# w_out in seven pairs by Strassen's products, its first fetches ahead of x's, block sums shared with GpSimd

## The chip, the cores and the metric

One core of one Trainium2 chip. The metric is the device time in microseconds of the program's one launch; lower is better. Engines are named as in the profile: PE (TensorE, matmuls), PEld (its weight loads), DVE (VectorE), ACT (ScalarE), POOL (GpSimd), SP (SyncE, which issues most DMAs).

## The reference

Talking-heads attention, and behind it a layer that normalizes `x @ w_in` and multiplies by `w_out`. The second half is what the change is about:

```
# q, k, v: 4 x 12 heads x 448 x 64; w_pre, w_post: 12 x 12
attn_out = attention(q, k, v, w_pre, w_post)
x = attn_out.transpose(0, 2, 1, 3).reshape(1792, 768)
h = x @ w_in                      # w_in: 768 x 1024
e = exp(h - max(h)); sm = e / sum(e)
solu = h * sm
ln = (solu - mean) / sqrt(var + 1e-6) * g_ln
out = ln @ w_out                  # w_out: 1024 x 768
```

All is float32 outside. Inside, a float32 matrix is the sum of two float16 ones, a high and a low half, and a product is three float16 matmuls (high x high, high x low, low x high).

## The kernel before, in words

The attention ends at about 430 us; its instructions stand in an order written by hand and are the same before and after the change. Behind it the program has 14 tiles of 128 tokens (`NT`), in the order of `TURNS` (11, 12, 13, 0 to 10), and seven pairs of tiles (`NPP`).

**Hidden product.** `hidden` (L1088) makes a tile's `x @ w_in` in 36 matmuls 128x512 into one of three PSUM banks `ps_h0` to `ps_h2`, tile t into bank t modulo 3. So tile 13 needs the bank of tile 10. VectorE takes a tile's maximum (L1711), ScalarE the exponent (L1722), VectorE the sum's reciprocal (L1733, L1736) and the product h x sm, `u` (L1739), which is the bank's last reader.

**Normalization.** ScalarE and small VectorE operations make the mean and the variance (L1751 to L1789), GpSimd a power (L1772). `ln_apply` (L1799, GpSimd) scales `u`, `ln_hi` (L1807, ScalarE) and `ln_lo` (L1811, GpSimd) split it into `lh` and `ll`, which go to DRAM (L1814) and come back transposed, `lt` (`turn`, L1826).

**w_out.** Eight fetches of 128 rows (`fetch_w_out`, DMA at L987) bring w_out as 64-bit words, issued by SP, between x's fetches `xf` (L974, L976). `convert_steps` turns each into float32: L1002, L1008, L1013, L1018 on VectorE, one step on ScalarE, the last, a product (L1021), on GpSimd. Then come maxima, one scale for all (`max_w_out`, `scale_w_out`), and the halves `wo_h` (ScalarE) and `wo_l` (VectorE, L377).

**Output product.** Of seven pairs, the first `NPL` = 2 are plain: four products of 24 matmuls 128x384 into banks `y`. The other five go by Strassen's algorithm: with both operands cut into 2 x 2 blocks, seven products of 12 matmuls replace eight blocks' worth, 84 in place of 96 a pair. For it VectorE adds the two halves of `lt` (`pair_whole`, L1841, `xs`), makes four block sums (`pair_sum`, L1854), and low halves (`part_lo`, L1663, `sz`); ScalarE makes the high halves. w_out's own block sums are `w_out_sum` (`tt`, `wo`) and their halves `tz`, also through the helper `minus` at L1663. `project` (L1903) issues the matmuls, into the `ps_h` banks for Strassen's products, and `emit` takes a product out of PSUM, scaled and added to what it belongs to (L1916 for the plain ones, L1935 for the others): nine VectorE operations and one on ScalarE a pair.

**What sets the order.** All of this is entered as tasks with engines, costs, due times and buffers (rings) into a planner, `moe`. `moe.order()` works greedily through them and its list is issued in that order, each engine's instructions in the order of the list. An instruction waits on its engine until what it reads is there.

Of the kernel before, what the change touches and what calls it, by code (L numbers as in the profile page):

```python
# [18 lines left out]
class Plan:  # L19
# [131 lines left out]
    def order(self):  # L151
# [94 lines left out]
def kernel(  # L246
# [748 lines left out]
    def convert_steps(dst, name):  # L995
# [24 lines left out]
        def product():  # L1020
            nc.gpsimd.tensor_tensor(out=dst, in0=z, in1=ex.bitcast(F32), op=ALU.mult)  # L1021
# [527 lines left out]
    with tc.manual_schedule():  # L1549
# [23 lines left out]
        wt_p = ctx.enter_context(tc.tile_pool(name="wt", bufs=1))  # L1573
        h_p = ctx.enter_context(tc.tile_pool(name="hp", bufs=2))
        cv_p = ctx.enter_context(tc.tile_pool(name="cv", bufs=2))
        lt_p = ctx.enter_context(tc.tile_pool(name="lt", bufs=2))
        sz_p = ctx.enter_context(tc.tile_pool(name="sz", bufs=2))
        ms_p = ctx.enter_context(tc.tile_pool(name="ms", bufs=3))
        ps_h = ctx.enter_context(tc.tile_pool(name="ps_h", bufs=1, space=PSUM))
        h_banks += [ps_h.tile([128, NF, 512], F32, name=f"ps_h{i}") for i in range(2)]  # L1580
        ps_y = ctx.enter_context(tc.tile_pool(name="ps_y", bufs=1, space=PSUM))
        ln_dr = [dram.tile([NT, 128, DFF], F16, name=f"ln_{z}") for z in "hl"]
# [10 lines left out]
        wo_h = wt_p.tile([128, KFF, DM], F16, name="wo_h")  # L1593
        wo_l = wt_p.tile([128, KFF, DM], F16, name="wo_l")
# [53 lines left out]
        NPP, NPL = NT // 2, 2  # L1648
        STEPS = [(i, j) for i in range(NPP) for j in range(4 if i < NPL else 7)]
# [575 lines left out]
```

## Time and profile before

| what | us |
|---|---|
| time, median of three runs | 636.11 |
| lowest and highest run | 635.67, 640.92 |
| the profiled execution's own time | 639.07 |
| its span on the core | 637.4 |

The profiled execution lies 2.96 us above the median; 1.67 us of it lie outside the span. Rows of the profile give a group's busy time, the mean duration of one instruction, and the idle time of its engine before it with the engine that ended it. In a row of the chain or of a timeline the first number is the start, the second the duration.

### The profile page before, as it was taken

The numbers are of one execution on the slowest core, as the hardware profiler recorded it, in microseconds if no ns is written. First come the engines' busy times: TensorE is split into PE (matmuls) and PEld (weight loads), VectorE is DVE, ScalarE is ACT, GpSimd is POOL, SyncE is SP. The second block draws the span as 40 slices with busy tenths as digits, with TensorE's granted clock in tenths as the row PEclk, the third lists the DMA queues.
The fourth block names the chain that finished last, engine by engine and source line by source line (L and its number), as shares of the span: only waits on it lengthen the run. The fifth ranks groups of instructions, "written<-read, shape, count | busy, mean of one in ns | idle before, by whom it ended". The sixth has DMA issues, their size and how long they took to land.

```text
span 637.4 us, 19852 instructions
## 1 busy us (share of the span) xinstructions
PE 607.9 (95%) x7674; PEld 409.0 (64%) x7674; DVE 542.8 (85%) x1293; ACT 453.1 (71%) x1022; POOL 289.8 (45%) x463
## 2 busy tenths in 40 slices
PE   7999989999899999999899998999999999999997
PEld 5757767777666776777577676764444445666664
DVE  4879988789797788997899898738999799999983
ACT  3879879998878888988799797625676688642110
POOL 2363584354673353862335426512678747510000
PEclk9999999999999999999899899999999999999999
DMA  8397288478877469889569762109994505571522
GB/s 195 117 203 222 97 179 228 158 197 202 236 176 185 167 187 186 252 194 230 181 189 197 235 215 90 37 4 347 273 249 112 148 35 132 157 176 50 115 79 72
DMA packets 135527, 106.81 MB, mean 168 GB/s; under 512 B 89508, under 2 KB 123400, under 8 KB 135432
## 3 DMA queue, kind: packets, MB, share of 16 engines
q1 hardware_dynamic: 129000, 91.36, 53.7%
q0 software_dynamic: 3712, 9.75, 6.3%
q10 hardware_dynamic: 2720, 4.42, 2.4%
q8 instruction: 61, 1.00, 0.7%
q14 instruction: 34, 0.28, 0.1%
HBM read 34.03 MB, written 16.97 MB: 80 GB/s over the span
## 4 chain that ended last, share of the span: by engine, by line
PE 63%; DVE 14%; DMA 7%; issue 5%; ACT 5%; POOL 4%; SPq 1%; POOLq 0%; DVEq 0%; ACTq 0%
PE ps_h L1088 13%; PE o L858 13%; PE ps_h L1903 11%; PE px L919 8%; PE ps L712 6%; PE pm L799 5%; PE y L1903 5%; DVE pm L811 4%; DVE s L735 3%; DMA sr<-s 2%; ACT e L827 2%; POOL wr L848 1%; DMA raw_v<-in_v_dram 1%; ACT s L730 1%; ACT p_t L381 1%
## 5 line engine op out<-in xcount | busy, mean ns | idle before, releaser
L858 PE MATMUL o<-wr,e 128*64 128x120 f32 x2520 | 161.3, 273 | 10.2 <-POOL wr L848 7.2
L858 PEld LDWEIGHTS o<-wr,e 128*64 128x64 f32 x2520 | 136.5, 138 | 44.3 <-POOL wr L848 23.5
L827 ACT ACTIVATE e<-pm,nb 128x448 f32<-128x448 f32 x180 | 114.6, 639 | 20.5 <-DVE pm L811 11.3
L811 DVE TENSOR_SCALAR_CACHE_REDUCE pm<-pm,c_nexp 128x448 f32<-128x448 f32 x171 | 113.5, 684 | 17.5 <-PE pm L799 15.3
L848 POOL TENSOR_SCALAR wr<-wq,sm 128x120 f32<-128x120 f32 x180 | 72.6, 411 | 105.3 <-DVE sm L842 66.7
L735 DVE SCALAR_TENSOR_TENSOR s<-ps,s 120x448 f16<-120x448 f32 (+1 forms) x180 | 105.7, 616 | 14.0 <-ACT s L730 11.5
L381 ACT COPY p_t<-o 128x480 f32<-128x480 f32 x180 | 107.8, 621 | 9.3 <-PE o L858 8.8
L730 ACT ACTIVATE s<-ps 120x448 f16<-120x448 f32 (+1 forms) x180 | 91.4, 551 | 21.0 <-PE ps L712 16.4
L919 PE MATMUL px<-p_t,raw_v 128*64 128x120 f32 (+3 forms) x1632 | 96.2, 259 | 0.3
L919 PEld LDWEIGHTS px<-p_t,raw_v 128*64 128x64 f32 x1632 | 83.6, 138 | 6.9 <-issue 6.0
L1088 PE MATMUL ps_h<-wi,xf 128*128 128x512 f16 x396 | 86.0, 379 | 0.8 <-DVE u L1739 0.8
L712 PE MATMUL ps<-k,q 64*64 64x448 f16 (+2 forms) x972 | 77.4, 355 | 6.1 <-DVE s L735 5.1
L1088 PEld LDWEIGHTS <-xf 128*128 128x128 f16 x396 | 38.8, 98 | 47.5 <-issue 1.1
L799 PE MATMUL pm<-sr,wp_hi 64*64 64x448 f16 (+1 forms) x684 | 56.5, 358 | 2.1 <-DMA sr<-s 1.6
L712 PEld LDWEIGHTS <-q 64*64 64x64 f16 (+2 forms) x972 | 33.4, 105 | 31.5 <-issue 21.1
L1903 PEld LDWEIGHTS <-lt 128*128 128x128 f16 x372 | 36.4, 98 | 24.2
L838 POOL TENSOR_SCALAR sm<-sm 128x2 f32<-128x2 f32 (+1 forms) x48 | 13.2, 276 | 69.4 <-ACT e L827 66.8
L827 ACT ACTIVATION_READ_ACCUMULATOR e<-pm,nb 128x1 f32 x180 | 37.3, 207 | 0.0
L1811 POOL TENSOR_TENSOR ll<-u,lh 128x1024 f16<-128x1024 f32 x14 | 32.0, 2284 | 11.4 <-ACT lh L1807 11.2
L377 DVE SCALAR_TENSOR_TENSOR xsl<-px,x_sc,xsh 128x120 f16<-128x120 f32 (+1 forms) x96 | 26.0, 326 | 12.4 <-ACT xsh L372 12.3
L799 PE MATMUL pm<-sr,wp_lo 64*64 64x448 f16 (+1 forms) x342 | 36.2, 349 | 0.0
L1903 PEld LDWEIGHTS <-sz 128*128 128x128 f16 x240 | 23.5, 98 | 15.5
(241 smaller groups left out, 1040.2 us busy)
## 6 DMA issues: line engine op xcount, KB each, us to landing
sr<-s SPq DMA_DIRECT2D x176, 210.0 KB
cv_wi<-in_moe_w_in_dram SPq DMA_DIRECT2D x24, 256.0 KB
cv_wo<-in_moe_w_out_dram SPq DMA_DIRECT2D x8, 768.0 KB
raw_k<-in_k_dram POOLq DMA_DIRECT2D x18, 224.0 KB, 4.6
raw_q<-in_q_dram POOLq DMA_DIRECT2D x18, 224.0 KB, 5.6
ln_h<-lh SPq DMA_DIRECT2D x14, 256.0 KB
ln_l<-ll SPq DMA_DIRECT2D x14, 256.0 KB
xh<-xsh SPq DMA_DIRECT2D x9, 224.0 KB
```

The lines of the kernel that those rows point to most:

```text
L381: nc.scalar.copy(out=out, in_=in_)
L712: nc.tensor.matmul(sps[b, c, h + e][lo:hi], q2[b, g][rows, 2 * j + x, i0 + lo : i0 + hi], k1[b, g][rows, 2 * j + y, 0:S], start=(a == 0), ...
L730: nc.scalar.activation(out=s_t[b, c][0 : y.shape[0], h, 0], in_=y, func=AF.Copy, scale=2.0**-E_S)
L735: nc.vector.scalar_tensor_tensor(out=t[:, h, 1], in0=y, scalar=2.0**-E_S, in1=t[:, h, 0], op0=ALU.mult, op1=ALU.subtract)
L799: nc.tensor.matmul(pmx[b, u + i][64 * e : 64 * e + 64, 0:S], w[rows], sr[b, u][rows, e, z], start=(a == 0), stop=(a == 2),)
L811: nc.vector.tensor_scalar(out=pmx[b, u][:, 0:S], in0=pmx[b, u][:, 0:S], scalar1=c, scalar2=None, op0=ALU.mult, op1=ALU.min, accum_out=nb,)
L827: nc.scalar.activation(out=ee[b, u], in_=pmx.pop((b, u))[:, 0:S], func=AF.Exp, bias=nbs.pop((b, u)), scale=-1.0, accum_out=sm,)
L848: ENG[eng].tensor_scalar(out=w, in0=wq[0:UK, 0 : H * UN], scalar1=sm, scalar2=1.0, op0=ALU.mult, op1=ALU.mult)
L858: nc.tensor.matmul(o_t[g][z * JH : (z + 1) * JH, c * 120 : (c + 1) * 120], e[:, x * JH : (x + 1) * JH], w, start=True, stop=True,)
L919: nc.tensor.matmul(xps[b, blk, g][e * 64 : e * 64 + 64, i, cut], raws["v", b, g][:, 2 * i + e, c * D : (c + 1) * D], next(x for y, x in bl ...
L1088: nc.tensor.matmul(ps[:, n], xx[:, kc, o : o + 128], ww[:, kc, n * 512 : (n + 1) * 512], start=(kc == 0 and a == 0), stop=(kc == KDM - 1 a ...
L1903: nc.tensor.matmul(y, x, w, start=(n == 0), stop=(n == len(terms) - 1 ))
```

## The change

- `NPL` is 0: all seven pairs go by Strassen's products. The products of neighbouring pairs are interleaved (`STEPS`). Their sums are in six banks: `ps_x`, `ps_y`, and four that take the place of the banks of `ps_h2` and `ps_h0` when these are closed; `ps_h1` stays for tile 13.
- The planner's greedy order is replaced by a stored table, `ORDER_MOE`: for every step the number of the task among those left, and, where it may run on two engines, which.
- The first four fetches of w_out stand ahead of x's fetches. The pools that hold w_out and the pairs are opened in another order, and a buffer used again waits for the tile that was in it (`reuse_waits="tile"`).
- Some tasks may now run on either of two engines: w_out's last product (GpSimd or VectorE), `ln_apply` (GpSimd or ScalarE), `ln_lo` (GpSimd or VectorE), `pair_whole`, `pair_sum`, `part_lo`, `w_out_sum` and the low halves of w_out's sums (VectorE or GpSimd). By the table 7 of 14 `ln_lo` are on VectorE, 6 of 14 `ln_apply` on ScalarE, 2 of 8 products on VectorE, and of the 14 `pair_whole`, 28 `pair_sum` and 14 `part_lo` 7, 16 and 7 on GpSimd.
- The left half of w_out's first four row blocks is split 384 wide, not 768.
- `emit` is arranged anew: seven VectorE operations and one on ScalarE a pair; a pair's second output tile lies in its `xs`.

```diff
+    ORDER_MOE = (
+        "0 1 16 46 1 0 0 30 3 54 1 4 0 0 27 30 7 0 20 9 1 1 27 0 0 18 42 20 3 7p 1 17 17 2 57 38 1 11 15 16 1 3 1 62 64 "
...
-    def stored(self):
-        if not self.ORDER:
+    def stored(self, order=None):
+        if not (order or self.ORDER):
...
-        def product():
-            nc.gpsimd.tensor_tensor(out=dst, in0=z, in1=ex.bitcast(F32), op=ALU.mult)
+        def product(eng="pool"):
+            ENG[eng].tensor_tensor(out=dst, in0=z, in1=ex.bitcast(F32), op=ALU.mult)
...
+        def pool(name, bufs):
+            return ctx.enter_context(tc.tile_pool(name=name, bufs=bufs, reuse_waits="tile"))
+
+        wh_p, cv_p, sz_p = pool("wh", 1), pool("cv", 2), pool("sz", 2)
+        wl_p, h_p, wt_p = pool("wl", 1), pool("hp", 2), pool("wt", 1)
+        lt_p, ms_p = pool("lt", 2), pool("ms", 3)
...
-        NPP, NPL = NT // 2, 2
-        STEPS = [(i, j) for i in range(NPP) for j in range(4 if i < NPL else 7)]
+        NPP, NPL = NT // 2, 0
+        STEPS = [(i, j) for i in range(NPL) for j in range(4)]
+        for i in range(NPL, NPP + 1):
+            STEPS += [x for x in ((i, 0), (i - 1, 1), (i, 3), (i, 2), (i - 1, 6), (i, 5), (i, 4)) if NPL <= x[0] < NPP]
...
-        def ln_lo(t):
+        def ln_lo(t, eng):
             x = lns[t, "l"] = h_p.tile([128, DFF], F16, tag="ll", name=f"ll_{t}")
-            nc.gpsimd.tensor_tensor(out=x, in0=us.pop(t), in1=lns[t, "h"], op=ALU.subtract)
+            minus(eng, x, us.pop(t), lns[t, "h"])
...
+        sums = {}
+
         def bank(i, j):
-            n = (7 * (i - NPL) + j) % 6
-            return h_banks[n % 3][:, n // 3, 0:DH]
+            n = sums["n"] = (sums.get("n", -1) + 1) % 6
+            for p, old in ((ph2, (2, 3)), (ph0, (4, 5))):
+                if n in old and old not in sums:
+                    p.close()
...
             work = {
-                1: lambda: [(py, px)],
-                3: lambda: [(px, px), (py, py)],
+                3: lambda: [(py, px)],
                 2: lambda: [(c(0, 0), px)],
-                4: lambda: [(c(1, 1), px), (px, px)],
-                5: lambda: [(c(1, 1), c(1, 1)), (c(1, 0), py)],
-                6: lambda: [(c(0, 1), px)],
+                5: lambda: [(pu, py)],
+                4: lambda: [(c(1, 1), pu), (py, py)],
+                1: lambda: [(c(1, 0), pu)],
+                6: lambda: [(c(0, 1), py)],
             }
...
-                {"sp": 0.65},
+                {"sp": 0.65} if kc > 3 else {"-": (0.0, 0.0)},
...
-        for _, e, _, run in moe.order():
+        for e, run in moe.stored(moe.ORDER_MOE):
             run(e)
```

On SP, behind the attention's last fetch `sr`, the order before is (`cv_wo` is a fetch of w_out, `xf` one of x, high and low half):

```order
L774 DMA sr_134<-s_3_6776 60x1x896 x2
L987 DMA cv_wo_7889<-in_moe_w_out_dram 128x1536
L987 DMA cv_wo_7941<-in_moe_w_out_dram 128x1536
L974 DMA xf_7943<-xh 128x2x512 x3
L1952 DMA g_sb<-in_moe_g_ln_dram 128x8x1
L987 DMA cv_wo_7951<-in_moe_w_out_dram 128x1536
L974 DMA xf_7943<-xl 128x2x512 x3
L987 DMA cv_wo_7961<-in_moe_w_out_dram 128x1536
```

After the change:

```order
L794 DMA sr_134<-s_3_6776 60x1x896 x2
L1007 DMA cv_wo_7898<-in_moe_w_out_dram 128x1536
L1007 DMA cv_wo_7900<-in_moe_w_out_dram 128x1536
L1007 DMA cv_wo_7902<-in_moe_w_out_dram 128x1536
L1007 DMA cv_wo_7904<-in_moe_w_out_dram 128x1536
L994 DMA xf_7965<-xh 128x2x512 x3
L994 DMA xf_7965<-xl 128x2x512 x3
```

Four of w_out's fetches now stand in front of all of x's; before, two did.

On VectorE, ahead of tile 10's product (`u_10`, the reader that frees tile 13's bank), the order before is:

```order
L1711 TENSOR_SCALAR u_10_8714,nb_10_8715<-ps_h0_7869,ch_7876 128x1024
L377 SCALAR_TENSOR_TENSOR wo_l_7881<-wo0_7957,gs_wo_7883,wo_h_7880 128x768 x2
L1841 TENSOR_TENSOR xs_2_8648<-lt_2_8615 128x1024
L377 SCALAR_TENSOR_TENSOR wo_l_7881<-wo0_7957,gs_wo_7883,wo_h_7880 128x768 x2
L1783 TENSOR_SCALAR z_9_8779<-y_9_8772,v_9_8731 128x1
L377 SCALAR_TENSOR_TENSOR wo_l_7881<-wo4_8189,gs_wo_7883,wo_h_7880 128x768 x2
L1789 TENSOR_SCALAR rs_9_8786<-z_9_8779,ch_7876,y_9_8772 128x1
L377 SCALAR_TENSOR_TENSOR wo_l_7881<-wo4_8189,gs_wo_7883,wo_h_7880 128x768
L1733 TENSOR_SCALAR sm_10_8777<-sm_10_8777 128x1
L1736 RECIPROCAL sm_10_8777<-sm_10_8777 128x1
L1739 SCALAR_TENSOR_TENSOR u_10_8714,su_10_8795<-ps_h0_7869,sm_10_8777,u_10_8714 128x1024
```

After the change (`ll` is a tile's low half, `tt` and `wo` w_out's block sums):

```order
L1687 TENSOR_TENSOR tt_0_8761<-wo0_7920 128x384
L1687 TENSOR_TENSOR ll_7_8767<-u_7_8511,lh_7_8759 128x1024
L1736 TENSOR_SCALAR u_10_8789,nb_10_8790<-ps_h1_7878,ch_7885 128x1024
L397 SCALAR_TENSOR_TENSOR wo_l_7890<-wo0_7920,gs_wo_7892,wo_h_7889 128x384
L1808 TENSOR_SCALAR z_9_8795<-y_9_8784,v_9_8782 128x1
L1687 TENSOR_TENSOR ll_8_8797<-u_8_8539,lh_8_8786 128x1024
L1814 TENSOR_SCALAR rs_9_8800<-z_9_8795,ch_7885,y_9_8784 128x1
L1758 TENSOR_SCALAR sm_10_8792<-sm_10_8792 128x1
L1761 RECIPROCAL sm_10_8792<-sm_10_8792 128x1
L1687 TENSOR_TENSOR wo4_8168<-wo4_8168,tt_0_8761 128x384
L1764 SCALAR_TENSOR_TENSOR u_10_8789,su_10_8815<-ps_h1_7878,sm_10_8792,u_10_8789 128x1024
```

Of the 768-wide halves `wo_l` and the add `xs_2`, which stood there, one `wo_l` 384 wide is left; low halves `ll` and sums of w_out stand there now.

On GpSimd the order of the same time before is:

```order
L1811 TENSOR_TENSOR ll_7_8644<-u_7_8487,lh_7_8639 128x1024
L1772 TENSOR_TENSOR y_8_8693<-v_8_8642,half_p_7884 128x1
L1799 TENSOR_SCALAR u_8_8567<-u_8_8567,rs_8_8712,nm_8_8717 128x1024
L1811 TENSOR_TENSOR ll_8_8728<-u_8_8567,lh_8_8723 128x1024
L1772 TENSOR_TENSOR y_9_8772<-v_9_8731,half_p_7884 128x1
L1799 TENSOR_SCALAR u_9_8628<-u_9_8628,rs_9_8786,nm_9_8789 128x1024
L1811 TENSOR_TENSOR ll_9_8840<-u_9_8628,lh_9_8798 128x1024
L1772 TENSOR_TENSOR y_10_8858<-v_10_8852,half_p_7884 128x1
L1799 TENSOR_SCALAR u_10_8714<-u_10_8714,rs_10_8873,nm_10_8876 128x1024
```

After the change:

```order
L1797 TENSOR_TENSOR y_8_8748<-v_8_8670,half_p_7893 128x1
L1687 TENSOR_TENSOR tt_0_8761<-wo4_8168,tt_0_8761 128x384
L1827 TENSOR_SCALAR u_8_8539<-u_8_8539,rs_8_8757,nm_8_8769 128x1024
L1797 TENSOR_TENSOR y_9_8784<-v_9_8782,half_p_7893 128x1
L1880 TENSOR_TENSOR xs_0_8465<-xs_0_8465 128x512
L1687 TENSOR_TENSOR tz_l_8778<-tt_0_8761,tz_h_8777 128x768
L1827 TENSOR_SCALAR u_9_8608<-u_9_8608,rs_9_8800,nm_9_8805 128x1024
L1687 TENSOR_TENSOR tt_1_8831<-wo0_7920 128x384
L1687 TENSOR_TENSOR tt_1_8831<-wo4_8168,tt_1_8831 128x384
L1687 TENSOR_TENSOR wo4_8168<-wo4_8168,tt_1_8831 128x384
L1880 TENSOR_TENSOR xs_0_8465<-xs_0_8465 128x512
```

GpSimd's low halves of tiles 7 to 9 are gone from it, and sums of w_out (`tt`, `wo4`, `tz_l`) and of pair 0 (`xs_0`) have come.

## Rows read from the trace of the kernel before

**Rows 1.** The page's part 1: busy us (share of span) x instructions.
```profile
PE 607.9 (95%) x7674; PEld 409.0 (64%) x7674; DVE 542.8 (85%) x1293; ACT 453.1 (71%) x1022; POOL 289.8 (45%) x463
```

**Rows 2.** The chain that ended last, 410 to 640: start, us, engine.
```profile
429.62 71.41 PE ps_h L1088 x330
...
515.66 3.07 DVE xs L1841
...
524.03 1.30 DVE u L1739 x2
...
525.38 7.93 PE ps_h L1088 x36
...
533.31 31.20 PE y L1903 x192
...
564.51 68.26 PE ps_h L1903 x420
...
632.80 0.62 DVE o L1935
```

**Rows 3.** Waits of PE, 430 to 638: us in total, times, longest.
```profile
PE ps_h L1088 <- DVE u L1739: 0.8, 1, 0.8
```

**Rows 4.** Windows: us, PE, PEld, DVE, ACT, POOL busy; clock; DMA share, GB/s.
```profile
420.00:430.00 10.00, 9.95 (x211) 7.18 (x209) 2.35 (x6) 0.97 (x2) 0.00 (x0) 1.00 0.01 2
...
440.00:450.00 10.00, 10.00 (x48) 4.56 (x47) 9.54 (x14) 6.63 (x13) 6.41 (x5) 1.00 1.06 330
...
430.00:525.00 95.00, 94.54 (x440) 42.95 (x438) 85.77 (x153) 64.41 (x126) 58.85 (x37) 1.00 0.71 196
...
525.00:558.00 33.00, 32.62 (x189) 18.49 (x189) 32.47 (x55) 25.58 (x47) 19.74 (x12) 1.00 0.54 141
```

**Rows 5.** Timeline, 503 to 512: start, us, engine, line.
```profile
505.52 2.13 POOL L1811 TENSOR_TENSOR ll<-u,lh 128x1024 f16<-128x1024 f32 x1 [1.43 <-ACT lh L1807]
...
505.72 3.01 DVE L1841 TENSOR_TENSOR xs<-lt 128x1024 f32<-128x1024 f16 x1 [1.21 <-DMA lt<-ln_l]
```

**Rows 6.** DVE by form, 430 to 638: busy, mean ns, idle before.
```profile
L1002 DVE TENSOR_SCALAR cv_wo<-cv_wo 128x768 uint32<-128x768 uint32 x8 | 9.1, 1164 | 0.9 <-DMA cv_wo<-in_moe_w_out_dram 0.9
...
L1008 DVE SCALAR_TENSOR_TENSOR cv_wo<-cv_wo 128x768 uint32<-128x768 uint32 x8 | 10.6, 1327 | 0.2 <-ACT cv_wo L1005 0.2
...
L1013 DVE TENSOR_SCALAR cv_wo<-cv_wo 128x768 uint32<-128x768 uint32 x8 | 9.2, 1145 | 0.2
```

**Rows 7.** Single lines, 430 to 638: ns min/median/max, first and last start.
```profile
L1841 DVE TENSOR_TENSOR xs<-lt x10: 1216/1222/3148, 505.7 to 607.9; 128x1024 f32<-128x1024 f16 x10
...
L1663 DVE TENSOR_TENSOR sz<-xs,sz x10: 1215/1215/2065, 533.9 to 618.6; 128x1024 f16<-128x1024 f32 x10
...
L1663 DVE TENSOR_TENSOR tt<-wo,tt x4: 559/1904/2471, 542.1 to 563.8; 128x384 f32<-128x384 f32 x4
...
L1002 DVE TENSOR_SCALAR cv_wo<-cv_wo x8: 546/932/2225, 433.8 to 491.1; 128x768 uint32<-128x768 uint32 x8
...
L1008 DVE SCALAR_TENSOR_TENSOR cv_wo<-cv_wo x8: 948/1136/2365, 436.9 to 494.6; 128x768 uint32<-128x768 uint32 x8
...
L1013 DVE TENSOR_SCALAR cv_wo<-cv_wo x8: 537/562/2545, 437.9 to 495.7; 128x768 uint32<-128x768 uint32 x8
...
L1811 POOL TENSOR_TENSOR ll<-u,lh x14: 2131/2242/2846, 445.6 to 558.4; 128x1024 f16<-128x1024 f32 x14
...
L1021 POOL TENSOR_TENSOR wo<-cv_wo x8: 1845/1852/2246, 439.9 to 499.0; 128x768 f32<-128x768 f32 x8
```

**Rows 8.** SP's timeline, 395 to 450, and its waits, 400 to 640.
```profile
429.19 0.81 SPq L987 DMA_DIRECT2D cv_wo<-in_moe_w_out_dram  x2
...
SPq L987 <- PE px L919: 29.6, 1, 29.6
```

**Rows 9.** PE's timeline, 420 to 640.
```profile
446.46 62.32 PE L1088 MATMUL ps_h<-wi,xf 128*128 128x512 f16 x288
```

More of the change, by code (lines that the diff above doesn't have):

```diff
@@ L1570 @@
         st.close()
[L1573 to L1580, printed above, removed]
+        def pool(name, bufs):
[3 more added lines that the diff above has]
+        lt_p, ms_p = pool("lt", 2), pool("ms", 3)
         ps_y = ctx.enter_context(tc.tile_pool(name="ps_y", bufs=1, space=PSUM))
+        ph2 = ExitStack()
+        for i, x in ((1, ctx), (2, ph2)):
+            ps_h = x.enter_context(tc.tile_pool(name=f"ps_h{i}", bufs=1, space=PSUM))
+            h_banks.append(ps_h.tile([128, NF, 512], F32, name=f"ps_h{i}"))
         ln_dr = [dram.tile([NT, 128, DFF], F16, name=f"ln_{z}") for z in "hl"]
@@ L1592 @@
         g_sb = wt_p.tile([128, KFF], F32, name="g_sb")
-        wo_h = wt_p.tile([128, KFF, DM], F16, name="wo_h")
-        wo_l = wt_p.tile([128, KFF, DM], F16, name="wo_l")
+        wo_h = wh_p.tile([128, KFF, DM], F16, name="wo_h")
+        wo_l = wl_p.tile([128, KFF, DM], F16, name="wo_l")
         c_out = wt_p.tile([128, 1], F32, name="c_out")
@@ L1836, in pair_whole @@
                 else:
-                    x = raw_p.tile([128, 2 * DFF + 2 * DH], F32, tag="raw", name=f"xs_{i}")
+                    x = raw_p.tile([128, 2 * DFF + DH], F32, tag="raw", name=f"xs_{i}")
                 xs[i] = x[:, 0 : 2 * DFF].rearrange("p (n f) -> p n f", n=4)
-                pz[i] = [x[:, 2 * DFF + n * DH : 2 * DFF + (n + 1) * DH] for n in range(2)]
+                pz[i] = x[:, 2 * DFF : 2 * DFF + DH]
             h, l = (lts[i][:, z, t].rearrange("p k f -> p (k f)") for z in range(2))
@@ L1979 @@
             add(("zM", kc), one(w_out_max, kc), {"act": (1.0, 1.1)}, after=prev, due=due + 8)
-        add(("zx", 0), max_w_out, {"dve": (0.2, 0.35)}, after=[("zM", kc) for kc in range(KFF)] + [("zg",)], due=70.0)
+        add(("zx", 0), max_w_out, {"dve": (0.2, 0.35)}, after=[("zM", kc) for kc in range(KFF)] + [("zg",)], due=55.0)
         add(
@@ L1989 @@
         )
[L1990 to L1991 removed]
+        add(("zx", 2), lambda e: o_steps[2][1](), {"dve": (0.2, 0.3)}, after=[("zx", 1)], due=55.0)
+        add(("zx", 3), scale_w_out, {"dve": 1.1}, after=[("zx", 2)], due=55.0)
         for kc in range(KFF):
@@ L2022 @@
                 )
-                add(("zL", x), lambda e, x=x: w_out_lo(x, e), {"dve": 1.0 * w}, after=[("zH", x)], due=due + d + 1)
+                add(("zL", x), lambda e, x=x: w_out_lo(x, e), {"dve": 1.0 * w, "pool": 1.7 if n == 2 else 0.9}, after=[("zH", x)], due=due + d + 1)
         for b in range(B - 1):
@@ L2137 @@
         T = TP
-        for n, (i, j) in enumerate(STEPS):
-            before = [STEPS[n - 1]] if n else []
+        for i, j in STEPS:
             a, b = 2 * i, 2 * i + 1
@@ L2153 @@
                 after=ready,
-                behind=[("zP",) + x for x in before] or [("zh", NT - 1)],
+                behind=[] if i >= NPL else [("zP", i, j - 1)] if j else [("zh", NT - 3)],
                 due=T,
@@ L2175 @@
                 on,
-                after=[("zP", i, j)],
-                behind=[("zE",) + x for x in before],
+                after=[("zP", i, j)] + ([("zE", i, x) for x in ((), (5,), (0,), (0,), (5,), (3,), (2, 3, 4))[j]] + ([("zL2", i, x) for x in range(2)] if j == 5 else []) + ([("zW", i, 0)] if j == 3 else []) if i >= NPL else []),
+                behind=[],
                 due=T - 12,
```

102 lines of the change are left out of this document (55 added, 47 removed), and 16 rows, old and new, of the table ORDER_MOE.

## The prediction

> **What bounds the kernel now.** I read the page's engine table first: TensorE is busy 607.9 of 637.4 us and VectorE 542.8 [rows 1]. So a gain must come from TensorE, and the question is who makes TensorE wait. The chain of waits answers it for the stage that the change touches [rows 2]: TensorE holds the chain without a break from 429.62 to 501.0, then VectorE for the last steps before 525.38, then TensorE again until 632.77 (564.51 + 68.26), after which one eviction and the last stores close the span. The list of TensorE's waits from 430 to 638 has a single row [rows 3]: 0.8 us, tile 13's hidden product, which waits until VectorE's product of tile 10 (L1739) lets its bank go. In the chain's TensorE rows a 128x384 output matmul takes 31.20/192 = 68.26/420 = 0.1625 us, whichever product it belongs to. The stretch ends 637.4 - 632.77 = 4.6 us after the last matmul, and the change leaves the form of these last steps alone.
>
> So this stage is TensorE's, but VectorE is only just in time: busy 85.77 of 95 us before tile 13 and 32.47 of 33 us from 525 to 558 [rows 4]. What it adds or loses there ends up as TensorE's wait.
>
> **What the change takes from TensorE.** Two pairs go from 96 output matmuls to 84: 24 x 0.1625 = 3.90 us. All of it lies on the path. If VectorE arrives in time at tile 13, the 0.84 us of that wait goes too: 4.74 us. I set the sum against the profiled execution, 639.07 us (span 637.4), which lies 2.96 us above the median of 636.11: 639.07 - 4.74 = 634.33, or 631.4 from the median. What follows is what VectorE and the queues give back.
>
> **Tile 13's bank.** Up to its release VectorE's queue in the kernel before takes 95.2 us (430.15 to 525.32). Of this 9.2 us are idle (95 - 85.77), and much of the rest is stretching: VectorE's operations that stay in SBUF are drawn out by GpSimd's. In [rows 5] GpSimd's low half runs 505.52 to 507.65, and VectorE's xs add, begun at 505.72, takes 3.01 us: it ends 1.08 us after GpSimd, and its shortest time is 1.216. The sum over the four lines concerned, mean against minimum [rows 6, 7]: L1002 8 x (1164 - 546) = 4.9, L1008 8 x (1327 - 948) = 3.0, L1013 8 x (1145 - 537) = 4.9, L1841 2 x 1.86 = 3.7 (its two in this stretch, 3.01 and 3.07, chain row 515.66 among them): 16.5 us. So 25.7 us are lost and 69.5 us are own work.
>
> The Trainium skill, page "SBUF — State Buffer", section "SBUF: two separate sides", speaks against this change: a VectorE operation with two SBUF inputs or in a two-port mode and a GpSimd operation on SBUF share one port pair, the first to start holds it for its whole instruction, and the other blocks. The 3.01 us row agrees with it.
>
> The new order puts this ahead of u_10 on VectorE (the second order fence): five low halves at 1.215 (the sz row, the same form, [rows 7]) = 6.1; two w_out products at the 0.95 of L1008's shortest (same width, two inputs) = 1.9; two 384-wide sums at 0.56 = 1.1; one 512-wide block sum, a little over half of an xs add, 0.7. It takes away one of the two xs adds, 1.2, and halves three of seven 768-wide wo_l, 3 x 0.48 = 1.4. Net +7.15: 76.7 us of own work. TensorE reaches tile 13 at 524.5, so there are 94.4 us, and 17.8 may be lost where 25.7 were. So 7.9 must be saved. What I find: five of the nine low halves that GpSimd ran there leave it (2.13 to 2.85 us each in [rows 7], all beside VectorE): five ninths of some 9.9 us of stretch, 5.5; two of eight GpSimd products (1.85), 1.4; the waits for w_out (0.9) and for the transposed fetch (1.2, [rows 5]), since w_out comes earlier and the first xs moves, 2.1. Against this GpSimd gets block sums and sums of w_out there: I give 2.5 back, one operation of 2.13 and a little. That is 6.5 of 7.9: tile 13 is **1.4 us late**. The ends are 0 (the gaps are filled wholly) and 7.9 (nothing is saved: low halves now on VectorE block against other GpSimd work as before). I take 1.4, since three of the six VectorE lines in [rows 7] (L1841, sz, L1013) have their median at their minimum: they collide only by chance of order.
>
> **The first products.** Before, they are plain and need no sums; now pair 0's sums and w_out's are needed from the start. Products start at about 532, each 12 x 0.1625 = 1.95 us. The tightest is pair 1's first product from its summed blocks, thirteenth in the new order: asked for at 532.3 + 12 x 1.95 + 1.4 = 557.1. After tile 10's product, at 525.9, VectorE's queue up to that low half holds four SoLU operations at 1.30 with their small ones, 5.7; tile 9's low half, 1.2; of w_out's sums and low parts thirteen at 0.55 (the tt row's shortest, 0.559) and two at 0.95, 9.05; two xs adds and two low halves at 1.22, 4.9; three 512-wide sums at 0.68, 2.0; five evictions at 0.62, 3.1; small ones, 0.5. That is 26.4 us, to 552.3. Of GpSimd's 58.85 busy us before tile 13 [rows 4] 16.5 were felt on VectorE, 28%; GpSimd's list here is 21.8 us (at 2.13 for a 1024-wide add, 1.07 for 512, 0.93 for 384, halves of the rows; none of before has these on GpSimd, and with 2.85 it would be 29). So 0.28 x 21.8 = 6.1 us of stretch, 558.4, **1.3 us late**. The ends: 0, if few meet. And if exclusion were whole, VectorE's 17.2 us that stay in SBUF and GpSimd's 21.8 would need 39.0 in the 33.2 from 524.5 to 557.7: 5.8 late. I take 1.3, the share that the rows show. Later products have 10 to 20 us of room; per pair VectorE's evictions fall from nine to seven at 0.62 [rows 2].
>
> **The fetches.** In the kernel before SP waits 29.6 us for an attention product before it issues w_out at 429.19 [rows 8], while the DMA engines stand at 2 GB/s [rows 4]. Four w_out fetches of 128 x 1536 words, 0.786 MB, now stand ahead of x's six transfers (first order fence). If they go out in the quiet time they cost nothing. If they still wait until 429, 3.1 MB of w_out and 1.57 MB of x need 14.3 us at 330 GB/s [rows 4]: 429.2 to 443.5, three us before the first matmul that uses x's fetch, 446.46 [rows 9]. At the 196 GB/s that is the mean of 430 to 525 it is 23.8 us, 453.0, and TensorE waits 6.5. I take 0, ends 0 and 6.5. The cover is the hidden product that ends at 446.46.
>
> The sum: 636.11 - 3.90 - 0.84 + 1.4 + 1.3 = **634.1 us** (by the profiled execution 637.0).
>
> **Rivals.** First, the vector queue stays late at tile 13: every low half that leaves GpSimd is paid for by new GpSimd work on the same operands. The wait is 7.9 us in place of 0.84, the time 636.11 - 4.74 + 7.9 = 639.3, slower than before (the products, asked for that much later, then wait no more); it decides from 4.74 us of wait. For it: VectorE is busy 85.77 of 95 us there, and gets 7.15 us more. Against: 9.2 us of idle time that better order can fill.
>
> Second, the first products wait the whole 5.8 us of the working above: 636.11 - 4.74 + 1.4 + 5.8 = 638.6. For it: 32.47 of 33 us busy already, with no sums of w_out due yet. Against: tile 13's own SoLU can wait, for its bank is not wanted.
> The same page's rule, taken as whole exclusion, is this rival; the trace bears it out only where two operations do meet: half of the VectorE lines in [rows 7] have their median at their minimum.
>
> Third, the change does less than it says, for the early fetches delay x by the 6.5 us: TensorE waits at 446 for x, and VectorE catches up meanwhile, so 631.4 + 6.5 = 637.9. For it: one queue, x behind w_out. Against: the idle DMA engines before 430.
>
> **How the numbers follow.** The forecast (waits of 0 to 4.7 us in all) 0.66, the first rival 0.15, the second 0.10, the third 0.05, and 0.04 for a gain that I don't see. About 1% is what a measurement can tell from no change: 629.7 to 642.5. Faster than that needs more than the 4.74 that TensorE can give: 0.04. Slower needs over 11.1 us of waits, the first two rivals together (7.9 + 5.8): somewhat over a quarter of their 0.25, 0.07. The rest, 0.89, is within. Range: from 631.4 less the 0.44 by which the lowest run lies under the median, 630.9, rounded to 630.8, up to the first rival's 639.3 with 0.7 of handover, 640.0. The forecast's own range is 630.8 to 636.1.
>
> **What would show it.** Right: 588 output matmuls at 0.1625 us without a gap, so that the output stretch takes 95.6 us where it took 99.5; waits of 0 to 3 us at tile 13 and as much at the thirteenth product; w_out's fetches in flight before 429; the summed maxima, low halves and adds of [rows 6] nearer their minima. Wrong: TensorE rows in the output stretch that name a low half or block sum as releaser with over 3 us in all (second rival); tile 13 with over 5 us behind L1739's successor (first); a wait of the hidden products for x at about 446 (third). The forecast falls if the time is above 636.

## The result and the profile after

The changed kernel takes 645.47 us (median of four runs, 642.42 to 648.87), the kernel before beside it 635.89 (632.52 to 640.92): a ratio of 1.0116, with a 95% interval of 1.0077 to 1.0155. It is slower by a little over 1%, where 634.1 was forecast.

The runs of the kernel before lie up to 8.4 us apart, those of the changed one 6.5, and the profiles say where from: the first matmul on x's fetch, behind the attention, starts at 446.46 us in the profile of before [rows 9] and at 443.44 in that of after, and between 442.47 and 451.05 in the eleven others, though the attention's instructions are the same in all. So I compare the stage that the change touches by itself, from this matmul to the end of the last one, in one profile of each kernel. Before it is 632.77 - 446.46 = 186.31 us long [rows 2, 9]. The window of exactly this stage, first in the kernel before, then in the changed one (length, then busy us of PE, PEld, DVE, ACT, POOL; granted clock, DMA):

```profile
446.46:632.77 186.31, 185.46 (x1011) 98.84 (x1009) 167.34 (x261) 97.07 (x178) 76.01 (x47) 1.00 0.52 133
```

```profile
443.44:636.78 193.34, 185.21 (x987) 97.16 (x985) 162.63 (x242) 108.42 (x195) 125.85 (x76) 0.98 0.54 132
```

The stage is 7.03 us longer. TensorE has 24 instructions less, and yet is busy as long as before; and it stands still for 193.34 - 185.21 = 8.13 us where it stood for 0.85. The list of its waits in the changed kernel from 440 to 660 (us in total, times, longest), which answers to [rows 3]:

```profile
PE s L1938 <- DVE o L1972: 6.2, 2, 4.0
PE spread_wo L363 <- DVE amx_wo L385: 1.9, 1, 1.9
```

TensorE's timeline shows where they are. There is no wait at tile 13 any more; there is one at the maximum of w_out (`spread_wo`), which is now issued between hidden tiles 8 and 9, and one at the ninth output product:

```profile
443.44 46.78 PE L1108 MATMUL ps_h<-wi,xf 128*128 128x512 f16 x216
492.11 0.46 PE L363 MATMUL spread_wo<-ident,amx_wo 128*128 128x128 f32 x2 [1.88 <-DVE amx_wo L385]
492.40 39.16 PE L1108 MATMUL ps_h<-wi,xf 128*128 128x512 f16 x180
531.40 0.33 PE L1938 MATMUL s<-wo_h,lt 128*128 128x384 f16 x1
...
549.45 0.34 PE L1938 MATMUL s<-wo_h,sz 128*128 128x384 f16 x1 [2.28 <-DVE o L1972]
...
584.59 0.48 PE L1938 MATMUL s<-wo_h,sz 128*128 128x384 f16 x1 [3.95 <-DVE o L1972]
584.86 0.52 PE L1938 MATMUL s<-wo_l,sz 128*128 128x384 f16 x1
```

The ninth product and the twenty-fourth (the third wait) each take the bank of the product six before, and that is free when VectorE has evicted it (`o`, L1972). VectorE's timeline has tile 10's product at 521.60, which frees tile 13's bank, then the two evictions at 548.79 and 583.93 with some of what stands ahead of them, and at 557.87 the low half that the thirteenth product reads:

```profile
521.60 1.27 DVE L1764 SCALAR_TENSOR_TENSOR u<-ps_h,sm,u 128x1024 f32<-128x1024 f32 x1
...
539.02 2.47 DVE L1687 TENSOR_TENSOR wo<-wo,tt 128x384 f32<-128x384 f32 x1 [1.17 <-POOL tt L1687]
...
547.65 1.21 DVE L1867 TENSOR_TENSOR xs<-lt 128x1024 f32<-128x1024 f16 x1
548.79 0.60 DVE L1972 SCALAR_TENSOR_TENSOR o<-s,c_out,o 128x384 f32<-128x384 f32 x1
...
557.87 1.21 DVE L1687 TENSOR_TENSOR sz<-xs,sz 128x1024 f16<-128x1024 f32 x1
...
579.31 1.64 DVE L1880 TENSOR_TENSOR xs<-xs 128x512 f32<-128x512 f32 x1
580.87 3.14 DVE L1867 TENSOR_TENSOR xs<-lt 128x1024 f32<-128x1024 f16 x1
583.93 0.60 DVE L1972 SCALAR_TENSOR_TENSOR o<-s,c_out,o 128x384 f32<-128x384 f32 x1
```

From 522.9 to 583.9 VectorE is idle almost only for results of GpSimd (1.40 and 1.17 us ahead of the first eviction, 1.16 ahead of the second, and 0.29 for ScalarE); the queue is simply late, with operations of 1.64, 3.14 and 2.47 us that take 0.68, 1.22 and 0.55 where they are shortest. By form, in the changed kernel from 443 to 640 (busy, mean ns), where [rows 7] have shortest times of 1216 and 1215 ns for the first and for the form of the last:

```profile
L1867 DVE TENSOR_TENSOR xs<-lt 128x1024 f32<-128x1024 f16 x7 | 13.7, 1965 | 0.0
L1880 DVE TENSOR_TENSOR xs<-xs 128x512 f32<-128x512 f32 x12 | 12.9, 1074 | 4.5 <-POOL xs L1880 4.4
L1687 DVE TENSOR_TENSOR ll<-u,lh 128x1024 f16<-128x1024 f32 x7 | 12.4, 1778 | 0.2 <-ACT lh L1833 0.2
```

And the clock. In windows of 2 us, behind the first wait, the second and the third:

```profile
492.00:494.00 2.00, 1.89 (x10) 1.09 (x11) 1.93 (x7) 1.20 (x2) 0.84 (x2) 1.00 0.75 252
...
550.00:552.00 2.00, 2.00 (x7) 0.88 (x6) 2.00 (x2) 0.00 (x0) 0.84 (x1) 0.50 0.00 0
...
584.00:586.00 2.00, 1.41 (x5) 0.69 (x5) 1.93 (x5) 0.00 (x0) 2.00 (x2) 0.50 0.24 92
```

Behind the waits of 2.28 and 3.95 us the granted clock is 0.50, the 1.2 GHz level, and the matmuls start 0.32 us apart where they start 0.16 apart at 2.4 GHz; behind the 1.88 us it stays at 1.00.

Ahead of the wait of 1.88 us at `spread_wo` the same is seen. Among the last steps that make w_out's last block is one on VectorE that takes 2.84 us where its form takes 0.95 at the shortest, 1.89 too much; a GpSimd add began just before it:

```profile
481.82 2.84 DVE L1028 SCALAR_TENSOR_TENSOR cv_wo<-cv_wo 128x768 uint32<-128x768 uint32 x1
```

```profile
481.71 2.14 POOL L1867 TENSOR_TENSOR xs<-lt 128x1024 f32<-128x1024 f16 x1
```

### The profile page after: what moved, and what is told of

It reads as the page before. It is cut to its first block, busy times and chain, and to the rows that moved or that the text cites. A ratio compares the mean times of both kernels' runs of the same rounds, so it can differ in the third digit from the quotient of the medians.

```text
span 640.7 us, 19817 instructions
## 1 busy us (share of the span) xinstructions
PE 605.5 (95%) x7650; PEld 406.0 (63%) x7650; DVE 538.6 (84%) x1273; ACT 462.3 (72%) x1033; POOL 338.1 (53%) x490
## 4 chain that ended last, share of the span: by engine, by line
PE 45%; DVE 25%; POOL 10%; DMA 8%; ACT 6%; issue 4%; SPq 0%; DVEq 0%; ACTq 0%; POOLq 0%
PE o L878 12%; PE s L1938 8%; PE px L939 7%; PE ps L732 6%; PE pm L819 5%; DVE pm L831 4%; DMA raw_v<-in_v_dram 4%; DVE s L755 3%; DMA sr<-s 3%; PE ps_h L1108 2%; POOL xs L1880 2%; POOL wr L868 1%; DVE u L1736 1%; DVE cv_wo L1028 1%; POOL u L1827 1%
## 5 line engine op out<-in xcount | busy, mean ns | idle before, releaser
L1938 PEld LDWEIGHTS <-sz 128*128 128x128 f16 x336 | 33.6, 100 | 30.3 <-issue 6.9
L1938 PE MATMUL s<-wo_h,sz 128*128 128x384 f16 x112 | 31.5, 348 | 6.2 <-DVE o L1972 6.2
L1938 PEld LDWEIGHTS <-lt 128*128 128x128 f16 x252 | 24.8, 98 | 16.7 <-issue 0.3
```

The costliest lines, as they stand in the source:

```text
L1938: nc.tensor.matmul(y, x, w, start=(n == 0), stop=(n == len(terms) - 1 ))
```

## Experiments

The experiments weigh one explanation, theory B, against others. Theory B: the change's work would fit, but VectorE and GpSimd hold each other out wherever VectorE works from SBUF, and the order fills both as if they didn't. Against it: the evictions only stand too deep in VectorE's queue (A); VectorE has too much to do, and sharing helps (A'); and, later, that no order can do without the plain pairs. In this table "stage" is as above, from the window of one profile of each kernel, in us; TensorE's idle time is its length less PE's busy time.

| kernel | ratio to before (95%) | stage | PE busy | PE idle | DVE busy | POOL busy |
|---|---|---|---|---|---|---|
| before | 1 | 186.31 | 185.46 | 0.85 | 167.34 | 76.01 |
| changed | 1.0116 (1.0077 to 1.0155) | 193.34 | 185.21 | 8.13 | 162.63 | 125.85 |
| evictions early | 1.006 (1.0026 to 1.0094) | 190.90 | 183.83 | 7.07 | 165.81 | 126.01 |
| sums on VectorE | 1.0069 (1.0048 to 1.0091) | 192.52 | 185.35 | 7.17 | 177.18 | 68.68 |
| both | 1.0062 (1.0025 to 1.0099) | 190.83 | 182.62 | 8.21 | 176.02 | 70.68 |
| low halves on GpSimd | 1.0249 (1.0199 to 1.0299) | 203.40 | 187.53 | 15.87 | 152.59 | 133.65 |
| two fetches late | 1.0155 (1.0121 to 1.019) | 195.06 | 185.49 | 9.57 | 164.33 | 125.78 |
| before, one plain pair | 1.0211 (1.0174 to 1.0248) | 198.84 | 187.03 | 11.81 | 175.01 | 75.93 |
| before, three plain pairs | 1.0049 (1.0021 to 1.0076) | 188.02 | 187.42 | 0.60 | 155.55 | 73.19 |
| before, GpSimd dosed | 1.0268 (1.0228 to 1.0307) | 201.83 | 188.44 | 13.39 | 183.33 | 98.83 |
| new order | 0.9917 (0.9883 to 0.995) | 181.42 | 181.40 | 0.02 | 141.17 | 112.25 |
| new order, second | 0.9892 (0.9847 to 0.9937) | 181.42 | 181.40 | 0.02 | 147.65 | 92.69 |
| blind order | 1.0094 (1.0054 to 1.0134) | 191.87 | 184.33 | 7.54 | 164.88 | 118.23 |

In the edits, `todo` is the order's list of (task, engine); `move(a, b)` puts task a in front of task b. `zE` is an eviction, `zW` the add of lt's halves, `zj` a block sum, `zL2` a pair's low half, `zo` a tile's low half, `zt` a sum of w_out, `zF` a fetch of w_out, `zX` one of x.

**Evictions early.**

```diff
+move(("zE", 0, 2), ("zt", 3, 2))
+move(("zE", 1, 2), ("zW", 1, 0))
+move(("zE", 0, 3), ("zW", 1, 0))
+move(("zE", 2, 2), ("zW", 1, 1))
+move(("zE", 3, 2), ("zj", 3, 1))
+move(("zE", 2, 1), ("zW", 4, 1))
+move(("zW", 4, 0), ("zW", 4, 1))
```

> Everything of the changed kernel, but eight of VectorE's steps change places: the evictions of products (0,2), (1,2), (0,3), (2,2) and (3,2) stand ahead of block sums and adds of lt that they stood behind, and the add of pair 4 stands behind three evictions. In the changed kernel TensorE waits 2.28 us at its ninth output product and 3.95 at its twenty-fourth, each for the eviction that frees its bank, and its clock is lower for some us behind each. Theory A (the evictions stand too deep in VectorE's queue): both waits go, and the time falls by 6.2 us and what the clock costs, about 8 in all, to some 637. Theory B (VectorE as a whole is late, since GpSimd's operations draw its own out; the place of an eviction only chooses who waits): the adds and sums behind the evictions are later by as much, and TensorE waits 4 us or more for a product's operand sz instead; the time stays within 3 us of the changed kernel.

Both waits for evictions went, and waits for operands came: TensorE's list now reads

```profile
PE s L1946 <- DVE sz L1695: 4.1, 2, 3.4
PE spread_wo L371 <- DVE amx_wo L393: 1.9, 1, 1.9
PE s L1946 <- ACT sz L1893: 1.1, 1, 1.1
```

Of the 8.13 us of idle time 7.07 are left. The stage is 2.44 us shorter, which is TensorE's clock (busy 1.38 us less) and 1.06 of waits. By the whole runs' ratios the gain is some 3.6 us, a little more than B's 3 and under half of A's 8. As B says: who waits was chosen, in the main, not whether. (The edit moves seven steps, not eight.)

**Sums on VectorE.**

```diff
+todo = [(k, "dve" if e == "pool" and k[0] in ("zW", "zj", "zL2") else e) for k, e in todo]
```

> The 7 adds of lt, 16 block sums and 7 low halves of pairs that GpSimd has in the changed kernel go to VectorE at the same places of the order. VectorE gets 7 x 1.22 + 16 x 0.68 + 7 x 1.22 = 28 us of own work, GpSimd loses some 57 us. Theory B (exclusion): each of these holds VectorE about as long on GpSimd as it takes on VectorE, so VectorE's busy time rises by far less than 28 us (under 15), the means of its xs<-lt, xs<-xs and sz fall from 1.97, 1.07 and 1.56 us to below 1.4, 0.8 and 1.3, and the time is within 4 us of the changed kernel or better. Theory A' (VectorE simply has too much to do and sharing helps it): busy time rises by 20 us or more, TensorE's waits grow by 10 us or more, and the time is over 655.

GpSimd's work fell by 57.2 us and VectorE's busy time rose by 14.6, not by the 28 of its own that came: 13.4 us of stretching went. The stage is no longer for it. So the sharing, on 30 operations of pairs, had bought nothing in this order. This is B's outcome, with VectorE's rise at the edge of what was expected (under 15). One size was missed: the mean of sz fell from 1.56 to 1.45 us only, not below 1.3 (xs<-lt to 1.30, xs<-xs to 0.74).

**Low halves on GpSimd.**

```diff
+todo = [(k, "pool" if k[0] == "zo" else e) for k, e in todo]
```

> The seven low halves ll that the change put on VectorE go back to GpSimd; nothing else moves. VectorE has 7 x 1.22 = 8.5 us less of own work, GpSimd 7 x 2.13 = 15 us more. Theory B (exclusion): VectorE's other operations are drawn out by as much or more; its busy time falls by under 4 us or rises, and the time is the same or up to 5 us longer, since ll also comes later. Theory A' (VectorE has too much own work): busy time falls by 8 us, TensorE's waits shrink by 3 us or more, time below 641.

A miss for both: VectorE's busy time fell by 10.0 us as A' has it, and yet the stage is 10.1 us longer, twice what B allowed. The seven low halves had taken 12.4 us on VectorE (the last row by form above), so its other operations grew by 2.4 us, beside 7.8 us more of GpSimd: less than B had. VectorE's list of waits shows where the time went:

```profile
DVE u L1744 <- POOL ll L1695: 14.4, 5, 4.8
```

The next tile's maximum waits for a buffer `u` until GpSimd has made the low half. It decides nothing on exclusion; it shows that an order holds for the engines it was made for.

**Two fetches late.**

```diff
+for i in range(6):
+    move(("zX", 0, i), ("zF", 2 + i // 3))
```

> The early fetches half undone: of the four fetches of w_out that stand ahead of x's, two stand behind three and six of x's first six transfers, as in the kernel before. If the early fetches are worth what the first steps of VectorE wait for w_out in the kernel before (0.9 us) or nothing, the time stays within 2 us of the changed kernel. If they cost something (they go out while the attention still runs), it is 2 us or more shorter; if they are what keeps VectorE from being later still, TensorE's waits grow by 3 us or more.

The stage is 1.72 us longer, 1.44 of it TensorE's idle time, and 0.78 us more are lost just ahead of it: the changed kernel has none of the 1.9 us in all that TensorE waits here at hidden tiles, for `u`. By the one profile the early fetches are worth 1.7 to 2.5 us in this order, which lies between two of the outcomes expected (the time within 2 us, or 3 us more of waits). They are not what costs.

**The kernel before with another number of plain pairs.**

```diff
-        NPP, NPL = NT // 2, 2
+        NPP, NPL = NT // 2, 1
```

> The kernel before with one number changed: six of seven pairs by Strassen's products (NPL 1 in place of 2), its planner making the order, nothing on other engines than before. TensorE has 12 output matmuls less, 1.95 us. Theory B says what the plain pairs do in the kernel before: their 31 us are the time in which VectorE makes w_out's sums and the first pair's. With 15.6 us of it gone VectorE, at 98% there, is late by what it can't find: TensorE waits 3 to 10 us for block sums, low halves or evictions, and the time is 1 to 8 us longer than before. The rival, that it is the changed kernel's sharing and its order alone that lose the time and one more pair by Strassen is a plain gain: no new waits, 1 to 2 us shorter than before.

Its stage is 12.5 us longer, more than the range; TensorE waits for the halves of w_out's sums, where B looked for it; that these lack the time beside the second plain pair is argued from it, and not shown by itself:

```profile
PE ps_h L1903 <- ACT tz_h L1693: 8.6, 3, 4.3
PE ps_h L1903 <- DVE tz_l L1663: 3.2, 3, 1.7
```

> The kernel before with four pairs by Strassen (NPL 3), its planner making the order. TensorE has 12 output matmuls more, 1.95 us. If VectorE's place beside the plain pairs is all that counts, nothing is gained from more of it, since TensorE waits only 0.84 us in this stage: 1 to 2 us longer than before. If the kernel before is itself short of that cover, the wait at tile 13 goes and the time is as before within 1 us.

With three plain pairs the stage is 1.71 us longer, the 1.95 of the matmuls less 0.25 of waits. Of one, two and three plain pairs two are best with this planner's order.

**GpSimd dosed.** In the kernel before:

```diff
             ENG[eng].tensor_tensor(out=out, in0=x, in1=y, op=op)
+            if i >= 4:
+                nc.gpsimd.tensor_tensor(out=scr, in0=wo_h[:, 4 + j], in1=wo_h[:, 4 + (j + 1) % 4], op=ALU.add)
```

> The kernel before with twelve more operations on GpSimd that nothing waits for and that share no data with others' work: beside each block sum of pairs 4 to 6 GpSimd adds two 128x768 float16 blocks of w_out's halves into a scratch tile. GpSimd is idle there in the kernel before. Theory B (a VectorE operation that stays in SBUF and a GpSimd operation exclude each other): GpSimd gets some 12 x 1.8 = 22 us, and VectorE's busy time rises by a third to two thirds of it, 7 to 14 us, its xs and sz operations of these pairs taking 1.5 to 3 us instead of 0.68 and 1.22, the evictions, which read PSUM, unchanged at 0.61; the time rises by 0 to 6 us, as VectorE has some room behind 580 us. The rival (GpSimd's work beside VectorE's is free but for chance): VectorE's busy time within 2 us of before, time the same.

The twelve additions, waiting for nothing but w_out, ran one behind another from 559.90 on, while VectorE made w_out's last sums, and not beside the sums of pairs 4 to 6 as expected. GpSimd's row (22.9 us busy, 1.91 a piece), then VectorE's in the same stretch, then VectorE's same operations in the kernel before:

```profile
559.90 23.73 POOL L1857 TENSOR_TENSOR scr<-wo_h 128x768 f16<-128x768 f16 x12
```

```profile
566.41 1.98 DVE L1664 TENSOR_TENSOR wo_l<-wo,wo_h 128x384 f16<-128x384 f32 x1
568.32 1.98 DVE L1664 TENSOR_TENSOR tt<-wo 128x384 f32<-128x384 f32 x1
570.33 1.87 DVE L1664 TENSOR_TENSOR tt<-wo,tt 128x384 f32<-128x384 f32 x1
...
575.95 2.38 DVE L1664 TENSOR_TENSOR tz_l<-tt,tz_h 128x768 f16<-128x768 f32 x1
578.25 0.60 DVE L1919 TENSOR_SCALAR o<-y,c_out 128x384 f32<-128x384 f32 x1
```

```profile
562.80 0.55 DVE L1663 TENSOR_TENSOR wo_l<-wo,wo_h 128x384 f16<-128x384 f32 x1
563.27 0.55 DVE L1663 TENSOR_TENSOR tt<-wo 128x384 f32<-128x384 f32 x1
563.85 0.56 DVE L1663 TENSOR_TENSOR tt<-wo,tt 128x384 f32<-128x384 f32 x1
...
565.39 0.95 DVE L1663 TENSOR_TENSOR tz_l<-tt,tz_h 128x768 f16<-128x768 f32 x1
566.25 0.61 DVE L1916 TENSOR_SCALAR o<-y,c_out 128x384 f32<-128x384 f32 x1
```

This is exclusion by itself: VectorE gets one operation that stays in SBUF done for each of GpSimd's. Operations of 0.55 us take 1.9 to 2.0, one of 0.95 takes 2.38, and the one that reads PSUM takes 0.60, as ever. It is not the DMA engines that draw them out: from 560 to 584 they were busy for 0.35 of the time here and 0.53 in the kernel before. VectorE's busy time rose by 16.0 us for 22.8 of GpSimd, 0.70 a us, above the expected third to two thirds; TensorE waited 7.49 and 5.10 us for w_out's sums, and the stage grew by 15.5 us where I had allowed 6.

**Both edits.** The lines of the first two experiments together.

> The changed kernel with both edits: the eight steps of the evictions moved ahead, and all of the pairs' adds, sums and low halves on VectorE. Alone, the first took the ratio to before from 1.012 to 1.006 and the second to 1.007. Theory B (VectorE is short of time, wherever its sums run): they don't add, since both leave VectorE its work: ratio 1.003 to 1.009. If lateness in the queue and exclusion are two separate losses, they add: ratio 1.000 to 1.002.

Ratio 1.0062, stage 190.83: as the first edit alone (190.90). They don't add.

**A new order.** If the order is at fault, one that reckons with exclusion must mend it. A search moved tasks about in the changed kernel's list, between the engines that the change allows too. Its durations were the shortest in the rows; a VectorE operation that stays in SBUF and a GpSimd operation held each other out, GpSimd from 0.45 us after its start, since beside its 128x1 powers, 0.541 us at the shortest, VectorE's operations can stay at their shortest (a product of 0.95 us beside the power of 446.56 in the changed kernel); and it wanted no wait of TensorE even with VectorE 12% slower and each hand-over three times as long. The edit is the table alone; its first lines:

```diff
     ORDER_MOE = (
-        "0 1 16 46 1 0 0 30 3 54 1 4 0 0 27 30 7 0 20 9 1 1 27 0 0 18 42 20 3 7p 1 17 17 2 57 38 1 11 15 16 1 3 1 62 64 "
+        "0 1 16 46 1 0 0 30 3 54 0 1 29 1 1 6 7 10 13 0 0 4 6 22 0 13 0 0 5 13 11 1 1 1 34 7 14 10 53 10 10 13 31 1 14 1 "
...
```

GpSimd keeps 8 of 14 adds of lt (before this 7), 19 of 28 block sums (16), 5 of 14 pair's low halves (7), 6 tile's low halves (7) and all eight products (6); ScalarE has 11 of 14 `ln_apply` (6).

> The changed kernel with nothing but another table of the order (and of who runs what, among the engines that the change allows). The table comes from a search that moves tasks about and keeps what ends earlier, with durations from the rows of the changed kernel's trace; its one rule beyond the change's planner is that a VectorE operation that stays in SBUF and a GpSimd operation hold each other out, as the rows with the twelve added operations showed. Theory B (the change's parts are sound, and its order is late because it doesn't reckon with exclusion): TensorE's three waits (1.88, 2.28, 3.95 us) and the clock that falls behind two of them go, 10 to 11 us in all: ratio to before 0.990 to 0.998. The rival (VectorE has too much to do with no plain pairs, whatever the order): waits come elsewhere, ratio 1.003 or more.

> A second table of the search with exclusion, from another start: 3 more of the adds of lt and 1 more of w_out's products are on VectorE or GpSimd than in the first. Theory B: as the first within 0.004 in ratio, 0.990 to 0.998; if the first table's time is chance of one order, they differ by more.

TensorE's list of waits is empty in both. Its timeline in the first:

```profile
448.55 46.78 PE L1107 MATMUL ps_h<-wi,xf 128*128 128x512 f16 x216
495.17 0.38 PE L362 MATMUL spread_wo<-ident,amx_wo 128*128 128x128 f32 x2
495.39 39.01 PE L1107 MATMUL ps_h<-wi,xf 128*128 128x512 f16 x180
```

and the windows of the stage in the first and the second:

```profile
448.55:629.97 181.42, 181.40 (x987) 96.51 (x985) 141.17 (x240) 111.09 (x194) 112.25 (x68) 1.00 0.55 138
```

```profile
444.35:625.77 181.42, 181.40 (x987) 96.47 (x985) 147.65 (x248) 111.32 (x196) 92.69 (x58) 1.00 0.56 141
```

Both beat the kernel before, by 0.8% and 1.1%; medians are 633.01 and 632.00 beside 638.67. The second's ratio, 0.9892, lies just under the range given for it and within 0.004 of the first. VectorE's busy time is 21.5 and 15.0 us under the changed kernel's, mostly stretching that went: in the second table VectorE even has six operations more than in the changed kernel (248 and 242 in the windows), with 17 of 28 block sums and 8 of 14 adds of lt, where the first gives it 9 and 6. So the rival that no order can do without the plain pairs falls, and with it A', that VectorE has too much to do.

Both tables also leave GpSimd less to do (112.25 and 92.69 us busy for 125.85), partly because ScalarE has 11 and 12 `ln_apply`. That alone is not what helps: "sums on VectorE" took more from GpSimd, down to 68.68 us, in the changed kernel's order, and TensorE still stood 7.17 us.

**The blind order.** The same search, from the same table and with the same margins, without the rule of exclusion (a shorter one: by its own rules the changed kernel's table had no wait to begin with).

> The same search with the same margins, started from the same table, but without the rule of exclusion. Theory B: this order is as late as the change's, since it fills VectorE and GpSimd as if they were free of each other: TensorE waits 5 to 10 us, ratio 1.008 to 1.020. The rival (any order with more slack does it, exclusion is not the point): as with the other table, 0.990 to 0.998.

```profile
PE s L1937 <- DVE xs L1971: 5.6, 1, 5.6
PE s L1937 <- ACT o L1959: 1.6, 1, 1.6
PE s L1937 <- POOL sz L1686: 0.4, 1, 0.4
```

7.54 us idle, ratio 1.0094: this order, made with margins and without the rule, is as late as the changed kernel's. TensorE is held up at another bank, and VectorE's and GpSimd's rows ahead of that eviction (565.31) show the rule that the search did without:

```profile
555.20 6.34 DVE L1879 TENSOR_TENSOR xs<-xs 128x512 f32<-128x512 f32 x3
...
565.31 0.60 DVE L1971 SCALAR_TENSOR_TENSOR xs<-s,c_out,o 128x384 f32<-128x384 f32 x1
```

```profile
554.07 1.87 POOL L1686 TENSOR_TENSOR tz_l<-wo,tz_h 128x384 f16<-128x384 f32 x1
556.02 4.98 POOL L1866 TENSOR_TENSOR xs<-lt 128x1024 f32<-128x1024 f16 x2
```

Three block sums of 0.68 us take 6.34 us beside three operations of GpSimd, 4.3 too much; TensorE's wait behind them is 5.59. What stays open is that this search was shorter than the other and that there is one order of its kind: how much of the difference of the tables is the rule and how much the longer search, these runs don't part.

## Why the prediction was wrong, step by step

- **TensorE's gain** was right. In the new orders, where nothing waits, the stage is 181.42 us, 4.89 under before; the sum had 4.74.
- **Tile 13.** The queue was forecast to free its bank at 525.9 on the clock of before; it did at 521.60 + 1.27 = 522.87 in a profile whose stage began 3.02 us earlier, which is 525.9. With ends of 0 and 7.9 us for what was put at 1.4, so close a hit is luck in part. The 1.4 us of wait did not show there, because TensorE had lost 1.88 us already at `spread_wo`. **That wait is a step I did not make**: the change moves it ahead by two hidden tiles, and TensorE stands in order behind the conversion of w_out's last block on VectorE, with the step of 2.84 us in it, and behind ScalarE's maximum. I counted what stands ahead on VectorE and SP, and not what TensorE itself stands behind.
- **The first products: the step that failed.** I took the thirteenth product, for its operand, as the tightest, 1.3 us late, and gave later ones "10 to 20 us of room". That room is the operands'. A product has a second condition, the bank: the ninth needs the third's eviction, which stands on VectorE behind w_out's sums, at 531.40 + 8 x 1.95 = 547.0, and it came at 549.39. The twenty-fourth was held up the same way, for 3.95 us. I had counted evictions as nine to seven, and five of them in VectorE's queue, and never as what frees a bank. The share of stretch, 28%, held up to there: from 522.9 to 548.8 the rows give 5.7 us beside 18.78 us of GpSimd, 30%, and 2.6 us more of waits for GpSimd's results, which I did not count. The thirteenth's low half, forecast for 558.4 on the clock of before, was there at 557.87 + 1.21 = 559.08, which is 562.1 on that clock; that its product did not wait for it is luck, since the ninth had held TensorE up by then. Behind that the share was too small: from 548.8 to 583.9 the five adds of lt and six block sums alone are 5 x 1.05 + 6 x 0.79 = 10 us over their shortest, beside 27.55 us of GpSimd, 36%.
- **The clock was left out.** PE's busy time is 185.21 us in place of 181.40: 3.81 us, nearly half as much again as the waits' 8.13.
- **The sum as measured:** matmuls -4.06 (181.40 - 185.46), idle time +7.28 (8.13 - 0.85), clock +3.81: 7.03 us, the stage's difference. Forecast were -3.90, +1.86 and nothing.
- **The rivals.** The second, whole exclusion at the first products, came nearest: 5.8 us of waits, where the output stage has 6.2. That is so in size alone: it had them at a low half or a block sum, and they came at evictions, 3.95 us of them at the twenty-fourth product. (By its own working there were 32.6 us up to the 557.1 at which the thirteenth is asked for, not 33.2, so it should have had 6.4.) I gave it 0.10 and no slow clock. None of the three signs of being wrong named an eviction. The Trainium skill, page "SBUF — State Buffer", section "SBUF: two separate sides", has the rule that of a VectorE operation with two SBUF inputs and a GpSimd operation that reads SBUF the first to start holds the shared ports for its whole instruction and the other blocks. The dosed rows agree that VectorE blocks. They don't agree that it is for the whole instruction: operations of 0.55 and 1.91 us, one after the other, would need 2.46 us a pair, and a pair took 1.9 to 2.0. GpSimd's twelve took 23.73/12 = 1.98 us apiece, little over their mean of 1.91, so there VectorE paid nearly alone.
- **The third rival** (x late) fell: w_out's four early fetches were issued by 397.9 us, in the quiet time, and no hidden product waited for x.

## What to carry to other kernels

Before VectorE's work is given to GpSimd, ask which of VectorE's operations stay in SBUF: beside those, GpSimd's time is in part VectorE's time (some 0.3 to 0.4 us a us where the two met now and then, 0.7 where both ran without a break), and an order that is to keep both busy should reckon with it. Where a matmul's result goes round a ring of banks, price the eviction as a deadline of its own, by its place in the queue, beside the operand's. A wait on TensorE can cost its own length and the slow clock behind it; compare stages, not whole runs, where something ahead of the change varies by more than the change.

## What was not expected of the hardware

GpSimd, given twelve operations in a row, kept its pace (1.98 us each) while VectorE fell to one operation for each of them; and a VectorE operation of 0.55 us and a GpSimd one of 1.91 fit together into 1.9 to 2.0 us, not 2.46, so a part of them lies outside the exclusion. GpSimd is not always the one that goes on: in the changed kernel its 128x1 power of 446.56 took 1.33 us, for 0.54 at the shortest, beside a VectorE product that kept its 0.95:

```profile
446.56 1.33 POOL L1797 TENSOR_TENSOR y<-v,half_p 128x1 f32<-128x1 f32 x1 [1.58 <-ACT v L1790]
```

```profile
446.52 0.95 DVE L1041 TENSOR_TENSOR wo<-cv_wo 128x768 f32<-128x768 f32 x1
```

The granted clock fell to 0.50 behind waits of 2.28 and 3.95 us and not behind one of 1.88. And the attention, with the same instructions, ended up to 8.6 us apart from one execution to another.
